# A linear-attention block gated by a squared-ReLU MLP: more matmuls on constants in the waits of the head

## The chip, the cores and the metric

The kernel runs on one core of a Trainium2 chip. The metric is device time in microseconds (us), the median of several executions; lower is better.

## The reference

One token sequence of 2048 rows and 448 columns, in bf16. It is normalised (layer norm without scale), and the result goes into two branches whose product is added to the input:

```python
xn = layernorm(x)                                   # x: 2048 x 448
q, k, v = split(xn @ wqkv)                          # 16 heads of 28
phi = lambda t: where(t > 0, t + 1, exp(t)) + 1e-6
kv  = einsum("bhsd,bhse->bhde", phi(k), v);  z = sum_s phi(k)
s   = (phi(q) @ kv) / (phi(q) @ z + 1e-6) @ wo
g   = silu(relu(xn @ w1 + b1) ** 2 @ w2 + b2)       # 448 -> 1792 -> 448
out = x + s * g
```

## The kernel before, in words

The rows are 16 tiles of 128 tokens, in four groups of four tiles. The kernel is a list of operations with the buffers that each reads and writes. A planner (`Program.schedule`) runs through them with a cost in us for each: TensorE (PE) and the DMA queue SP keep the order of the list; VectorE (DVE), ScalarE (ACT) and GpSimd (POOL) are ordered by the planner's due times, and some of their operations may go to either of two engines. The planner also gives each PSUM buffer (`Buf`) one of the eight banks, the one that is free first. Then each engine gets its instructions with the semaphore waits that the buffers ask for.

The body of the work, from about 13 us on, is a stream of PE matmuls: H (`hh`, line 786: xn times w1, per group and 128 hidden columns), K and Q (lines 729 and 739), G (lines 1092 and 1109: squared hidden times w2), and the attention's small products. The change is ahead of that, in the head, where PE waits for the first tiles:

- DMAs bring x of tile 0 (SP), tile 1 (ACT's queue), tiles 2 and 3, then w_k in four pieces, then w1 in three column ranges (0 to 511, 512 to 1279, 1280 to 1791; each as one main transfer and two for the last 64 rows), x of tiles 4 to 7 after the second, then w_q.
- Layer norm of a tile: DVE statistics (`ln_stats`, lines 483 and 484, giving `st` and `mv`), ACT Ln and Exp (`ln_rstd`, lines 491 and 495), DVE subtract and scale (`ln_norm_first` for tile 0 in two pieces, line 503; `ln_norm`, line 525), giving `xn`.
- PE transposes of xn against an identity (`pe_transpose`, line 602), in pieces of up to three blocks of 128 columns, each copied out of PSUM to `xT` by ACT (line 613) or DVE (line 612). The last 64 columns of two tiles go together (`pe_transpose_rests`, lines 627 and 637).
- K of tiles 0 and 1 in parts (`k_part`, line 801, one matmul of 128x448 for each block; `k_rests`, line 816, for the last 64 columns), and the first two hidden blocks of group 0 in parts (`head_part`, line 829; `head_rest`, line 845). `bias_cols` (line 1234) transposes b1.
- The matmuls on constants: `warm(n, after)` multiplies `dum`, a 128x128 tile of zeros, by itself n times into a PSUM bank of its own that nobody reads. With `after` the group waits for the buffers named. The planner counts 0.075 us for each.

The order of PE in the head is the order of these calls:

```python
warm(30)
warm(4, [("mv", 0)])
pe_transpose(0, ((0, 1, "act"), (1, 3, "dve")))
k_part(0, 0, 1)
k_part(0, 1, 3)
pe_transpose(1, ((0, 3, "act"),))
pe_transpose(2, ((0, 3, "dve"),))
k_part(1, 0, 3)
```

After them come the transposed rests of tiles 0 and 1, the bias, `head_part` on tiles 0 and 1, the transposes of tile 3, `k_rests`, the rests of tiles 2 and 3, `head_part` on tiles 2 and 3, `head_rest`, and then the stream of line 786.

Of the kernel before, what the change touches and what calls it, by code (L numbers as in the profile page):

```python
# [46 lines left out]
class Program:  # L47
# [6 lines left out]
    def add(self, eng, emit, reads=(), writes=(), dur=0.2, alts=(), nbytes=0, mode=None, label="", slow=1.0):  # L54
        op = Op(eng, emit, reads, writes, dur, alts, nbytes, mode, label)
        op.slow = slow
        for t in op.reads:
            op.raw.add(self.writer[t])
            self.readers.setdefault(t, []).append(op)
        for t in op.writes:  # L60
            w = self.writer.get(t)
            if w is not None and w is not op:
                op.deps.add(w)
            for r in self.readers.get(t, ()):
                if r is not op:
                    op.deps.add(r)
            self.writer[t] = op
            self.readers[t] = [r for r in self.readers.get(t, ()) if r is op]
        op.raw.discard(op)
        op.deps |= op.raw  # L70
        for d in op.deps:
            d.succ.append(op)
        self.ops.append(op)
        return op
# [231 lines left out]
def bass_recurrent_scan__linear_attn_block__dense_activation_squared_relu__prompt_kernel(  # L306
    nc, A_x, A_wqkv, A_wo, B_x, B_w1, B_b1, B_w2, B_b2, out
):
    with ExitStack() as es:
# [28 lines left out]
        mv = sb("mv", [P, NT, 2], f32)  # L338
# [255 lines left out]
        def pe_transpose(si, pieces):  # L594
            for lo, hi, eng in pieces:
                b = Buf("T")

                def f(e, _, lo=lo, hi=hi, b=b):
                    v = ps(b)[:, :].bitcast(bf)
                    last = None  # L600
                    for c in range(lo, hi):
                        last = e.transpose(v[:, (c - lo) * P : (c - lo + 1) * P], xn[:, si, c * P : (c + 1) * P], ident[:, :])
                    return last

                src = ("xf" if (si, hi) == (0, 1) else "xn", si)
                add("pe", f, [src, "ident"], [b], 0.0558 * (hi - lo), mode="128", label=f"T{si}.{lo}")

                def ev(e, eng, lo=lo, hi=hi, b=b):
                    src = ps(b)[:, 0 : 64 * (hi - lo)].bitcast(bf)
                    dst = xT[:, si, lo:hi, :].rearrange("p c k -> p (c k)")  # L610
                    if eng == "dve":
                        return e.tensor_copy(dst, src)
                    return e.activation(out=dst, in_=src, func=AF.Copy)

                n = hi - lo
                add(
                    eng, ev, [b], [("xT", si, c) for c in range(lo, hi)],
                    0.15 + 0.07 * n if eng == "dve" else 0.18 + 0.107 * n, label=f"eT{si}.{lo}",
                ).prio = -30
# [178 lines left out]
        def k_part(si, lo, hi):  # L798
            def f(e, _):
                for c in range(lo, hi):  # L800
                    last = e.matmul(  # L801
                        ps(k_head[si])[:, 0:D], xT[:, si, c, :], w_k[:, c, :], start=(c == 0), stop=False, skip_group_check=True
                    )
                return last

            add(
                "pe", f, [("wk", c) for c in range(lo, hi)] + [("xT", si, c) for c in range(lo, hi)] + ([k_head[si]] if lo else []),
                [k_head[si]], (hi - lo) * MM(D), mode="128", label=f"K{si}.{lo}",
            )
# [403 lines left out]
        def warm(n, after=()):  # L1213
            b = Buf("W")

            def f(e, _):
                last = None
                for _i in range(n):
                    last = e.matmul(ps(b)[:, 0:P], dum[:, 0:P], dum[:, 0:P], start=True, stop=True)
                return last  # L1220

            add("pe", f, ["dum", *after], [b], n * 0.075, mode="128", label="warm")
# [13 lines left out]
            )  # L1236
            add("act", lambda e, _: e.activation(out=b1f[:, :], in_=ps(bb)[:, 0 : NF // 2].bitcast(bf), func=AF.Copy), [bb], ["b1f"], 0.2, label="b1f")

        warm(30)
        warm(4, [("mv", 0)])  # L1240
        pe_transpose(0, ((0, 1, "act"), (1, 3, "dve")))
        k_part(0, 0, 1)
        k_part(0, 1, 3)
        pe_transpose(1, ((0, 3, "act"),))
        pe_transpose(2, ((0, 3, "dve"),))
        k_part(1, 0, 3)
        pe_transpose_rests(0)
# [135 lines left out]
```

## Time and profile before

| | |
|---|---|
| median of 3 runs | 147.61 us (147.25 to 147.79) |
| the profiled execution | 147.9 us, of which the span of its instructions is 146.1 |
| PE busy | 140.1 us (96%), 1177 matmuls |
| DVE, ACT, POOL busy | 102.4 (70%), 80.2 (55%), 6.3 us (4%) |
| DMA | 12.89 MB, mean 88 GB/s |
| mean granted clock of PE | 0.988 |
| chain that ended last | PE 91%, DVE 4%, DMA 2%, ACT 1% |

The span is the time from the first to the last instruction in one profiled execution. Start times below are us from its beginning. "PEclk" is the share of PE's full clock that was granted. A matmul's duration includes its way through the array, so back-to-back matmuls overlap in the records: their spacing, not their duration, is what each costs. Rows of DMAs give the time from issue to landing.

### The profile page before, as it was taken

To read this page: it belongs to the slowest core of one execution; us is meant where nothing else is said; L and a number is where in the kernel's file an instruction comes from. 1 tells how busy PE (TensorE), PEld (TensorE's weight loads), DVE (VectorE), ACT (ScalarE), POOL (GpSimd) and SP (SyncE) were. 2 spreads that over 40 slices of the span, in tenths; PEclk is the share of its full clock that TensorE was granted. 3 is DMA by queue.
4 is the path that set the end of the run, shared out by engine and by line. 5 is a ranking of instruction groups with operands and counts; after the bars stand their busy time and mean duration, and the time that the engine had idled before them with its cause. 6 is when DMAs were issued, how large, how long until landed. Compare 5 with 4: busy or idle time off the path is not lost.

```text
span 146.1 us, 3000 instructions
## 1 busy us (share of the span) xinstructions
PE 140.1 (96%) x1177; PEld 70.0 (48%) x1177; DVE 102.4 (70%) x222; ACT 80.2 (55%) x148; POOL 6.3 (4%) x40
## 2 busy tenths in 40 slices
PE   7599999999999999999999999999999999999991
PEld 7355444554444444444444444444546455555471
DVE  0943999879678899939789788963032745874874
ACT  3447997304488735597878557888417540301311
POOL 7900000000000000000000000000000000000000
PEclk9969999999999999999999999999999999999999
DMA  4899994559233100132200000000397000323032
GB/s 142 232 236 291 300 349 103 82 113 303 49 52 51 27 0 0 18 49 45 36 4 0 0 0 0 4 0 11 105 215 191 8 0 7 98 87 99 31 116 73
DMA packets 23515, 12.89 MB, mean 88 GB/s; under 512 B 14290, under 2 KB 22734, under 8 KB 23502
## 3 DMA queue, kind: packets, MB, share of 16 engines
q1 hardware_dynamic: 21842, 11.46, 30.7%
q10 hardware_dynamic: 1660, 1.25, 3.6%
q8 instruction: 9, 0.15, 0.5%
q14 instruction: 4, 0.03, 0.1%
HBM read 9.23 MB, written 1.90 MB: 76 GB/s over the span
## 4 chain that ended last, share of the span: by engine, by line
PE 91%; DVE 4%; DMA 2%; ACT 1%; issue 0%
PE pb L786 28%; PE pb L1109 19%; PE pb L1092 7%; PE pb L1184 7%; PE pb L887 6%; PE pb L729 6%; PE pb L739 6%; PE pb L1149 3%; DMA x_tok<-in_A_x_dram 2%; PE pb L829 2%; PE pb L866 1%; DVE st L483 1%; DVE gbuf L1173 1%; PE pb L893 1%; PE pb L1036 1%; PE pb L801 1%
## 5 line engine op out<-in xcount | busy, mean ns | idle before, releaser
L786 PE MATMUL pb<-xT,w 64*128 64x512 bf16 x378 | 43.6, 376 | 0.0
L764 ACT ACTIVATE r<-pb,b1f 128x512 bf16<-128x512 f32 x39 | 25.3, 685 | 15.4 <-PE pb L786 15.3
L786 PEld LDWEIGHTS pb<-xT,w 64*128 64x128 bf16 x378 | 18.0, 94 | 22.6 <-issue 1.1
L1109 PE MATMUL pb<-w,r 128*128 128x448 bf16 x140 | 27.7, 353 | 0.0
L1109 PEld LDWEIGHTS pb<-w,r 128*128 128x128 bf16 x140 | 13.2, 98 | 13.9 <-issue 1.2
L776 ACT ACTIVATE r<-r 128x1024 bf16<-128x1024 bf16 x17 | 17.8, 1062 | 0.7 <-DVE r L761 0.5
L761 DVE TENSOR_SCALAR r<-pb,b1f 128x512 bf16<-128x512 f32 x17 | 12.4, 746 | 6.0 <-PE pb L786 6.0
L1082 DVE TENSOR_TENSOR gbuf<-pb,b2b 128x448 bf16<-128x448 f32 x14 | 8.5, 618 | 5.8 <-PE pb L1109 4.3
L1204 DVE TENSOR_TENSOR gbuf<-pb,gbuf 128x448 bf16<-128x448 f32 x14 | 8.1, 618 | 6.1 <-PE pb L1184 6.1
L1092 PE MATMUL pb<-w,r 64*128 64x448 bf16 x112 | 11.7, 349 | 0.0
L729 PE MATMUL pb<-w_k,xT 64*128 64x448 bf16 x98 | 11.6, 349 | 0.0
L739 PE MATMUL pb<-xT,w_q 64*128 64x512 bf16 x84 | 11.0, 376 | 0.0
L483 DVE BATCH_NORM_STATS2 st<-x_tok 128x6 f32<-128x448 bf16 x16 | 9.1, 608 | 2.6 <-DMA x_tok<-in_A_x_dram 2.6
L1132 ACT ACTIVATE gbuf<-gbuf 128x448 bf16<-128x448 bf16 x14 | 7.0, 570 | 6.8 <-DVE gbuf L1082 5.9
L1184 PE MATMUL pb<-w_k,pqT 64*128 64x448 bf16 x96 | 10.5, 349 | 0.0
L887 PE MATMUL pb<-pk,xn 128*128 128x448 bf16 x48 | 9.6, 353 | 0.0
L1000 DVE TENSOR_TENSOR pqT<-pqT,xT 128x2048 bf16<-128x2048 bf16 x3 | 3.7, 1223 | 8.2 <-DMA xT<-scr 8.2
L719 DVE SCALAR_TENSOR_TENSOR pk<-pb,pk 128x448 bf16<-128x448 f32 x16 | 9.3, 617 | 0.1
L923 DVE TENSOR_TENSOR zacc<-zacc,pk 128x448 f32<-128x448 f32 x13 | 8.1, 620 | 0.2
L712 DVE TENSOR_SCALAR pk<-pk 128x448 bf16<-128x448 bf16 x16 | 4.1, 274 | 5.7 <-ACT pk L707 5.6
L707 ACT ACTIVATE pk<-pb 128x448 bf16<-128x448 f32 x16 | 7.8, 545 | 0.6 <-PE pb L729 0.6
L1092 PEld LDWEIGHTS pb<-w,r 64*128 64x128 bf16 x112 | 5.4, 94 | 5.3 <-issue 0.4
(99 smaller groups left out, 142.3 us busy)
## 6 DMA issues: line engine op xcount, KB each, us to landing
out_dram<-gbuf SPq DMA_DIRECT2D x15, 112.0 KB, 1.7
w<-in_B_w_dram SPq DMA_DIRECT2D x1, 1568.0 KB, 10.4
x_tok<-in_A_x_dram SPq DMA_DIRECT2D x3, 448.0 KB, 6.6
xT<-gbuf SPq DMA_DIRECT2D x32, 32.0 KB, 2.0
w<-in_B_w_dram SPq DMA_DIRECT2D x2, 384.0 KB, 5.8
xT<-scr SPq DMA_DIRECT2D x6, 112.0 KB
w<-in_B_w_dram SPq DMA_DIRECT2D x1, 576.0 KB, 6.6
xT<-scr ACTq DMA_DIRECT2D x5, 112.0 KB
```

The costliest lines, as they stand in the source:

```text
L483: add("dve", lambda e, _: e.bn_stats(st6[:, si, :], x_tok[:, si, :]), [("x", si)], [("st", si)], 0.61, label=f"bn{si}").prio = hp(si, 0)
L719: lambda e, _: e.scalar_tensor_tensor(out=slot, in0=ps(buf)[0:rows, 0:n], scalar=1.0 + 1e-6, in1=slot, op0=ALU.add, op1=ALU.max),
L729: return e.matmul(ps(b)[:, 0:D], x_tile(rows, si, c), w_k[rows, c, :], start=start, stop=stop)
L739: return e.matmul(ps(b)[:, 0:512], w_q[rows, c, m * P : (m + 1) * P], x_group(rows, g, c), start=start, stop=stop,)
L761: return e.tensor_scalar(out=slot, in0=ps(b)[:, 0:512], scalar1=b1f[:, fi : fi + 1], scalar2=0.0, op0=ALU.add, op1=ALU.max)
L764: return e.activation(out=slot, in_=ps(b)[:, 0:512], func=AF.Relu, bias=b1f[:, fi : fi + 1])
L776: return e.activation(out=both, in_=both, func=AF.Square)
L786: return e.matmul(ps(b)[:, 0:512], w_1[rows, c, fi * P : (fi + 1) * P], x_group(rows, g, c), start=start, stop=stop,)
L887: last = e.matmul(ps(b)[:, 0:D], xn_cols(si, c * P, (c + 1) * P), pk[:, si, :], start=(si == 0), stop=(si == NT - 1),)
L1092: return e.matmul(ps(b)[:, 0:D], r_cols(rows, fi, si), w_2[rows, fi, :], start=start, stop=stop)
L1109: last = e.matmul(ps(b)[:, 0:D], r_cols(slice(0, P), fi, si), w_2[:, fi, :], start=(fi == 0), stop=(fi == NF - 1),)
L1184: return e.matmul(ps(b)[:, 0:D], w, msb[rows, c, :], start=start, stop=stop)
```

## The change

Two of the groups of constant matmuls get longer, and two more groups are put into the head: 35 in place of 30 at the start, 7 in place of 4 behind the statistics of tile 0, 4 between the first and the second part of K of tile 0, and 6 between the transposes of tile 1 and those of tile 2. `warm` itself is as it was.

```diff
-        warm(30)
-        warm(4, [("mv", 0)])
+        warm(35)
+        warm(7, [("mv", 0)])
         pe_transpose(0, ((0, 1, "act"), (1, 3, "dve")))
         k_part(0, 0, 1)
+        warm(4)
         k_part(0, 1, 3)
         pe_transpose(1, ((0, 3, "act"),))
+        warm(6)
         pe_transpose(2, ((0, 3, "dve"),))
         k_part(1, 0, 3)
```

## The prediction

> **What bounds the kernel now.** I read the page first, then busy time by stretch, then the timeline of the head, then the transfers. The page's slices show TensorE (PE) full nearly everywhere and its granted clock full nearly everywhere, with one dip:
>
> ```profile
> PE   7599999999999999999999999999999999999991
> ...
> PEclk9969999999999999999999999999999999999999
> ```
>
> A slice is 3.65 us. PE is the end of the chain (91% of it), so what delays PE in the head delays the end. The 6 in the third slice is where the change works. Busy time by stretch, cut where the clock changes (quarter-microsecond stretches put the fall at 8.19 and the rise at 11.60, 3.41 us apart; I cut the other stretches to the same grid):
>
> ```profile
> core 0: us, PE busy (x) PEld busy (x) DVE busy (x) ACT busy (x) POOL busy (x), PEclk, DMA share, GB/s
> 1.36:4.78 3.42, 3.08 (x29) 2.81 (x27) 1.16 (x3) 1.28 (x1) 3.22 (x23) 1.00 0.77 211
> 4.78:8.19 3.41, 1.82 (x13) 0.88 (x13) 3.19 (x11) 2.27 (x9) 2.23 (x12) 1.00 0.88 233
> 8.19:11.60 3.41, 3.38 (x18) 2.12 (x18) 0.92 (x4) 1.05 (x5) 0.00 (x0) 0.50 0.91 256
> ...
> 141.31:144.72 3.41, 1.88 (x21) 1.59 (x19) 2.12 (x8) 1.13 (x3) 0.00 (x0) 1.00 0.36 119
> ```
>
> The clock is the number after POOL. PE is hardly idle at half clock (3.38 of 3.41 us): there it is the limit, and the stretch can cost at most half of itself, 1.71 us. The stretch before it is the loose one. The timeline of PE (start, duration, instruction, count, idle before and releaser):
>
> ```profile
> 1.06 3.38 PE L1219 MATMUL pb<-dum 128*128 128x128 bf16 x30 [1.06 <-DVE dum L368]
> 5.01 0.40 PE L1219 MATMUL pb<-dum 128*128 128x128 bf16 x4 [0.57 <-DVE mv L484]
> 5.97 0.23 PE L602 MATMUL pb<-ident,xn 128*128 128x128 bf16 x1 [0.57 <-DVE xn L503]
> ...
> 6.59 0.35 PE L801 MATMUL pb<-w_k,xT 128*128 128x448 bf16 x1
> 7.14 0.55 PE L801 MATMUL pb<-w_k,xT 128*128 128x448 bf16 x2 [0.20 <-DVE xT L612]
> 7.53 0.33 PE L602 MATMUL pb<-ident,xn 128*128 128x128 bf16 x3
> 8.22 0.50 PE L602 MATMUL pb<-ident,xn 128*128 128x128 bf16 x3 [0.36 <-DVE xn L525]
> 8.51 1.33 PE L801 MATMUL pb<-w_k,xT 128*128 128x448 bf16 x3
> ...
> 10.11 1.46 PE L829 MATMUL pb<-xT,w 128*128 128x256 bf16 x6
> 11.36 0.45 PE L602 MATMUL pb<-ident,xn 128*128 128x128 bf16 x3
> ...
> 12.40 0.83 PE L829 MATMUL pb<-xT,w 128*128 128x256 bf16 x6
> 13.16 0.39 PE L845 MATMUL pb<-xT,w 64*128 64x512 bf16 x2
> ```
>
> The same six matmuls take 1.46 us at half clock and 0.83 at full. The 30 constant matmuls stand (3.38 - 0.31) / 29 = 0.106 us apart, the four at 5.01 (0.40 - 0.22) / 3 = 0.06: so PE really ran at half until about 4.78 (the column has no record before), was granted full speed for one stretch, lost it at 8.19 and had it again at 11.60.
>
> **The change, part by part.** No instruction of DVE, ACT, POOL or a DMA is added or moved; only PE gets work, in four waits.
>
> *35 for 30.* The 35th starts at 1.06 + 34 x 0.106 = 4.66 and ends by 4.98; the next group waits for the statistics of tile 0 until 5.01. Cost 0.
>
> *7 for 4.* Three more at 0.056 end at about 5.58; the first transpose waits for DVE until 5.97. Even at half clock they end at 5.96. Cost 0.
>
> *4 inside K of tile 0.* K's first matmul at 6.59 streams for 0.19 (two take 7.53 - 7.14 = 0.39), so the four run 6.78 to 7.00; K goes on at 7.14, when DVE has copied the rest of xT. Cost 0, spare 0.14.
>
> *6 ahead of the transposes of tile 2.* The transposes of tile 1 stream from 7.53 to 7.70, the six to 8.03; tile 2's wait for DVE's normalised rows until 8.22. Cost 0, spare 0.19. If these covers are gone (half clock), see the last rival.
>
> *Banks and order.* Two more groups take a PSUM bank each for a moment. By the list, five of the eight banks have been used when the group of 4 comes and seven when the group of 6 does, so both find a fresh one; the buffers behind them then take the banks of older fillers or of copies long done. Were one behind a copy that still runs, it would cost up to 0.2 (tile 1's copy ends at 8.38, tile 2's transposes start at 8.22). The planner counts 0.075 us for each constant matmul, and could settle DVE and ACT differently later on; I bound that by 0.7 either way (one Relu of line 764, of 0.685, earlier or later) and take 0, since the waits swallow the fillers in its plan as they do here.
>
> *The clock.* Is 4.78 to 8.19 now full enough? Counted by spacing, before it holds 4 x 0.056 constants, 6 x 0.056 transposes and 3 x 0.19 of K: 1.13 us, 33%, and the clock fell after it. The other partly filled stretch, 141.31 to 144.72, holds by spacing some 1.6 us, 48% (PE is done issuing at 142.94), and the clock did not fall after it. So, if one limit governs both, it lies between 33% and 48%. The change adds 13 x 0.056 = 0.73: 1.86 us, 54%, above it. By the page's modelled busy time the bracket is 1.82 to 1.88 us and the new value about 2.5, above it too.
> The Trainium skill (TensorE: Matmul & The Clock Gate, Part 4: PE-mode transpose) says that transposes do not count as busy in the same way. By that the new fill would be 1.52 us, 45%, inside a bracket of 23% to 48%; no row here separates the two, and the sum goes by the plain count.
>
> *What full clock from 8.19 is worth.* Transposes of tile 2 at 8.22 for 0.18; K of tile 1 from 8.44 (ACT's copy ends at 8.38) for 3 x 0.19, to 9.01; transposed rests and bias to 9.3 (before: 9.63 to 10.11, 0.48 at half; I take 0.29); six of line 829 for 0.66, to 9.97 (before 10.11 to 11.36); then tile 3's transposes at 9.97 in place of 11.36. From there the chain over ACT to line 829 takes about what it takes now (11.36 to 12.40 less some 0.12 for the half-clock transposes, so 0.92): 10.89 in place of 12.40. **1.51 us earlier**; the bound was 1.71.
>
> *What is late next.* After line 845 come eight matmuls of line 786 on the first piece of w1, then those on its second piece. The issues of its three transfers, in the timeline of SP:
>
> ```profile
> 5.73 1.77 SPq L427 DMA_DIRECT2D w<-in_B_w_dram  x3
> ```
>
> and the median time from issue to landing of the last two, in the list of DMAs:
>
> ```profile
> w<-in_B_w_dram SPq DMA_DIRECT2D x2, 96.0 KB, 6.2
> ```
>
> The third is issued at about 5.73 + 2 x 0.59 = 6.9 and lands at about 13.1. Now its first use is at 13.38 + 8 x 0.108 = 14.25, with 1.15 to spare. With 1.51 taken off it would come at 12.74, so PE waits 0.36 for it. The transfers start by SP's own pace and do not come earlier. **Kept: 14.25 - 13.1 = 1.15 us.** The third piece of w1 (in the trace it lands at 16.2; first used 48 matmuls later, at about 19.4) and w2 (lands at 23.1, used at 25.45) have room; the layer-norm of tiles 4 to 7 (14.91) is fed by a DMA and may move less than PE, but is for a use at 36.
>
> Sum: the profiled execution took 147.9 us, its span 146.1 and 1.8 around it. 147.9 - 1.15 = 146.75. It lies 0.3 above the median, so the median of 147.61 becomes 146.5.
>
> **The rivals.**
> *The clock falls all the same.* Then every filler is hidden and nothing is gained: 147.6 (147.4 to 147.9). For it: the limit may not be one fill for all places, or transposes may not count. Against: the 48% stretch.
> The Trainium skill (TensorE: Matmul & The Clock Gate, Why this matters for your kernels) asks only for no idle gap over about 3 us. By that the gaps here are no cause and fillers no cure; the trace disagrees, since the longest gap in 4.78 to 8.19 is 0.57 and the clock fell.
> *The clock holds, but the gain is lost again*, in a later wait such as the PSUM banks in the stream of line 786, where ACT and DVE are 80 to 90% busy: a gain of 0.4 to 0.7, so 146.9 to 147.2.
> *The clock holds and w1 lands in time:* the whole 1.51, 146.1.
> *Slower: the fillers run at half clock.* If the stretch up to 4.78 is not enough to raise the clock, everything stays at half until 11.60. Then K's first matmul ends at 6.97, four fillers of 0.106 at 7.40 (0.26 late), K's two at 8.14, the transposes at 8.46 and six fillers at 9.10: tile 2's transposes come 0.88 late, of which half is got back once the clock rises. Plus 0.44 to 0.88: 148.0 to 148.5. It decides if the grid of stretches falls so that the constants fill only part of one. Against: 84% fill sufficed here, and the four runs lie within 0.65 us.
> The Trainium skill (same page, Part 1: The HAM clock gate) calls that grid free-running, not tied to the kernel's start; one trace cannot show it.
>
> **How the numbers follow.** 0.5% of 147.61 is 0.74 us, about what a measurement of this kernel can tell from no change. Clock holds and 1.15 is kept: 0.55. Whole 1.51: 0.08. Both are faster: 0.63. Holds but lost again: 0.09, and falls all the same: 0.17, both within 0.5%: 0.26. Slower: 0.11. The range reaches from the whole gain, 146.0, to the clock falling all the same, 147.8; it leaves out the slower case and some edges. The likeliest case by itself is 146.1 to 146.8.
>
> **What would show it.** Right: granted clock 1.00 from 8.19 on and the third slice at 9; six matmuls of line 829 at about 9.3 in 0.83; tile 3's transposes near 10.0; an idle time of PE of some 0.36 before line 786 that a DMA of w ends, near 13.1; 145 as span. Wrong: a stretch at 0.50 anywhere in the first 15 us, tile 2's transposes later than 8.25, or idle time of PE before line 786 ended by ACT or DVE.

## The result and the profile after

The changed kernel takes 146.81 us (median of 7 executions, 146.6 to 147.21) against 147.61 for the kernel before (147.25 to 148.5). The ratio is 0.9946, 95% interval 0.992 to 0.9971: 0.5% faster. The profiled execution took 147.21 us with a span of 145.0 (before: 147.9 and 146.1). All ratios here leave out executions that lie more than 1.5% above the fastest of their kernel (four of the kernel before, one of the start-only kernel); medians and counts keep them.

The page's slices, PE busy and granted clock, no longer have the dip in the third slice:

```profile
PE   7998999999999999999999999999999999999991
...
PEclk9999999999999999999999999999999999999999
```

The timeline of PE in the head:

```profile
1.05 4.66 PE L1219 MATMUL pb<-dum 128*128 128x128 bf16 x42 [1.05 <-DVE dum L368]
5.64 0.79 PE L602 MATMUL pb<-ident,xn 128*128 128x128 bf16 x3
6.29 0.36 PE L801 MATMUL pb<-w_k,xT 128*128 128x448 bf16 x1
6.49 0.39 PE L1219 MATMUL pb<-dum 128*128 128x128 bf16 x4
6.82 0.55 PE L801 MATMUL pb<-w_k,xT 128*128 128x448 bf16 x2
7.21 0.33 PE L602 MATMUL pb<-ident,xn 128*128 128x128 bf16 x3
7.37 0.50 PE L1219 MATMUL pb<-dum 128*128 128x128 bf16 x6
7.90 0.34 PE L602 MATMUL pb<-ident,xn 128*128 128x128 bf16 x3
...
9.02 0.83 PE L829 MATMUL pb<-xT,w 128*128 128x256 bf16 x6
9.68 0.33 PE L602 MATMUL pb<-ident,xn 128*128 128x128 bf16 x3
...
11.58 1.03 PE L786 MATMUL pb<-xT,w 64*128 64x512 bf16 x8
13.11 2.12 PE L786 MATMUL pb<-xT,w 64*128 64x512 bf16 x18 [0.51 <-DMA w<-in_B_w_dram]
```

All 42 constants run 0.107 apart, so at half clock; the first K at 6.29 is the first matmul at full clock (0.36 us, as in the profile before). Tile 3's transposes come at 9.68 in place of 11.36, and then the stream of line 786 stops for the second piece of w1, which lands at 13.07. That is the only wait of PE after 8 us, in the list of waits (total, times, longest):

```profile
PE pb L786 <- DMA w<-in_B_w_dram: 0.5, 1, 0.5
```

From 13.11 on PE is some 1.13 us earlier than before (where the same matmul, the ninth of line 786, ran at 14.25; the last matmul of all comes at 141.82 in place of 142.94), which is the 1.1 us of the spans. DVE, ACT and SP have the same instructions in the same order as before.

One thing differs from the picture of the prediction: here the clock rose at 6.31, not at 4.78. The edges of the stretches lie elsewhere: 6.31 is 1.54 us after 4.78, and a stretch is 3.41 long. Ten more profiles below rise at ten other places. So one profile of the kernel before shows one case of several, and the experiments had to look at many executions. In the tables below, a mean clock of 0.988 marks an execution in which the clock rose and fell again for one stretch (0.5 x 3.41 / 146 = 0.012). Half clock ahead of the first rise is not in that mean (the record begins with the rise); it shows in the spacing of matmuls and in the span.

### The profile page after: what moved, and what is told of

The parts are those of the page before. It is cut to its first block, busy times and chain, and to the rows that moved or that the text cites. A ratio compares the mean times of both kernels' runs of the same rounds, so it can differ in the third digit from the quotient of the medians.

```text
span 145.0 us, 3036 instructions
## 1 busy us (share of the span) xinstructions
PE 140.3 (97%) x1195; PEld 70.9 (49%) x1195; DVE 102.2 (70%) x222; ACT 80.2 (55%) x148; POOL 6.6 (5%) x40
## 4 chain that ended last, share of the span: by engine, by line
PE 88%; DMA 4%; SPq 4%; DVE 1%; issue 0%
PE pb L786 28%; PE pb L1109 19%; PE pb L1092 7%; PE pb L1184 7%; PE pb L887 6%; PE pb L729 6%; PE pb L739 6%; DMA w<-in_B_w_dram 4%; SPq L427 4%; PE pb L1149 3%; PE pb L866 1%; DVE gbuf L1173 1%; PE pb L893 1%; PE pb L1036 1%; PE pb L961 1%; PE pb L1062 1%
## 5 line engine op out<-in xcount | busy, mean ns | idle before, releaser
L1109 PEld LDWEIGHTS pb<-w,r 128*128 128x128 bf16 x140 | 13.1, 98 | 13.9 <-issue 1.2
L719 DVE SCALAR_TENSOR_TENSOR pqT<-pb,pqT 128x512 bf16<-128x512 f32 x12 | 7.7, 681 | 0.0
```

The source lines that it names most:

```text
L719: lambda e, _: e.scalar_tensor_tensor(out=slot, in0=ps(buf)[0:rows, 0:n], scalar=1.0 + 1e-6, in1=slot, op0=ALU.add, op1=ALU.max),
L1109: last = e.matmul(ps(b)[:, 0:D], r_cols(slice(0, P), fi, si), w_2[:, fi, :], start=(fi == 0), stop=(fi == NF - 1),)
```

## The experiments

The runs below fall into three sets, each compared with executions of the kernel before from the same set: 29, 29 and 23, together 81, median 147.63. In the column of the clock one execution of the kernel before at 0.985 is counted with those at 0.988.

| kernel | executions | mean clock 0.988 | span 146.4 or more | span 145.4 or less |
|---|---|---|---|---|
| before (30, 4) | 81 | 25 | 19 | 9 |
| changed (35, 7, 4, 6), two runs | 17 | 0 | 0 | 16 |
| start only (35, 7), two runs | 18 | 0 | 1 | 15 |
| 35 and 4 only | 12 | 5 | 1 | 5 |
| middle only (30, 4, 4, 6) | 12 | 0 | 0 | 8 |
| middle as transposes | 12 | 1 | 0 | 3 |
| no constants at all | 12 | 0 | 6 | 0 |

### The longer start alone

```diff
-        warm(30)
-        warm(4, [("mv", 0)])
+        warm(35)
+        warm(7, [("mv", 0)])
```

> 35 and 7 constant matmuls, none in the middle. Theory A (a stretch of the clock's grid falls back to half when it is filled too little, and the fillers of the middle lift it): the middle is as loose as before (with 7 for 4 the stretch 4.78 to 8.19 would be filled 39% by spacing, against 33%), so half-clock stretches stay in most executions: mean clock 0.985 to 0.995, 147.0 to 147.7 us. Rival B (what pays is the longer start, which raises the clock surely by about 4.8 or 6.3): clock 0.998 or more and the whole gain, 146.8 us.

Measured: 146.79 us, ratio 0.9934 (0.9908 to 0.9961), no execution at 0.988. The whole gain, and this was rival B's number, not mine. Six executions were few, so it ran again in the third set:

> 35 and 7 at the start and nothing in the middle, once more, for more executions. Open is whether the fillers of the middle do anything beside the longer start. With 7 the loosest stretch after a rise (4.78 to 8.19) is filled to 38% by spacing; stretches of 32 and 33% let the clock fall, 48 and 49% held it. If the limit lies under 38%: no execution at a mean clock of 0.988, 146.8 us as in the first such run, and the middle is not needed. If it lies above: some of ten executions show 0.988 and spans of 145.8, median up to 147.2 us.

Measured: 146.94 us, ratio 0.9944 (0.9918 to 0.997), again none at 0.988. One of these 12 has a span of 147.2 at a clock of 0.998, longer than the 146.7 that the latest rises below give; the kernel before has one such too, and what made them is open. The middle's fillers are not needed beside the longer start, as far as 18 executions show; a difference between the two kernels of less than about 0.2% would not show here.

### The middle alone

```diff
         k_part(0, 0, 1)
+        warm(4)
         k_part(0, 1, 3)
         pe_transpose(1, ((0, 3, "act"),))
+        warm(6)
         pe_transpose(2, ((0, 3, "dve"),))
```

> 4 and 6 constant matmuls in the middle, 30 and 4 at the start as before. Theory A: no half clock after the first rise when the grid lies as in the profile of before: clock 0.997 or more, 146.8 to 147.1 us; where the grid lies as in the profile of after (edges at 2.90 and 6.31), 30 and 4 fill 2.90 to 6.31 to only some 54% and the rise may come a stretch later. Rival B: no gain, 147.5 us.

Measured: 147.08 us, ratio 0.9962 (0.9935 to 0.9989), none at 0.988, but four of 12 spans over 145.4. Its profile caught one of those (span 145.9). The timeline of PE:

```profile
5.03 0.61 PE L1219 MATMUL pb<-dum 128*128 128x128 bf16 x4 [0.59 <-DVE mv L484]
...
7.00 0.63 PE L1219 MATMUL pb<-dum 128*128 128x128 bf16 x4
7.43 0.95 PE L801 MATMUL pb<-w_k,xT 128*128 128x448 bf16 x2
8.18 0.53 PE L602 MATMUL pb<-ident,xn 128*128 128x128 bf16 x3
8.50 0.85 PE L1219 MATMUL pb<-dum 128*128 128x128 bf16 x6
9.14 0.53 PE L602 MATMUL pb<-ident,xn 128*128 128x128 bf16 x3
...
10.60 0.83 PE L829 MATMUL pb<-xT,w 128*128 128x256 bf16 x6
```

Everything is at half clock until 9.97. This is the delay of the prediction's slower rival, tile 2's transposes at 9.14 in place of 8.22; but with 147.68 us this execution takes no longer than the kernel before does in the median. The stretch from 3.15 to 6.56 held the end of the 30, the four and two transposes, 50% by spacing, and the clock did not rise after it. So two things cost time in the kernel before: a fall after a loose stretch, and a late rise. The middle heals the fall (none at 0.988 in 12 executions, against 25 of 81); the longer start heals both.

### Which part of the start

```diff
-        warm(30)
+        warm(35)
         warm(4, [("mv", 0)])
```

> 35 in place of 30, the 4 and the middle as before. By the limits that the runs so far leave, the five more make the rise earlier in part of the executions (fewer spans of 146.6 and more), but the stretch of 4.78 to 8.19 stays at 33 to 34%, as loose as the one that let the clock fall: 0.988 in a quarter of the executions or more, median 147.3 us (147.0 to 147.6). If the three more behind the statistics do nothing: as with 35 and 7, 146.8 us.

Measured: 147.59 us, ratio 0.9982 (0.9951 to 1.0012), five of 12 at 0.988, as expected, and slower than the 147.3 that I put on it. So it is the three more constants behind the statistics of tile 0 that keep the clock: 5 of 12 with 4, none of 12 with 7 in the same set (none of 18 in both). By spacing they would lift the stretch 4.78 to 8.19 from 33% to 38%. No kept profile has a stretch as loose as that with the clock held: the two of the start-only kernel hold 52 and 66% in the first stretch after their rises, and an execution meets the loosest one only at some positions of the grid.

### No constants

Both calls of `warm` are left out.

> No constant matmuls at all. Theory A2: PE's first work comes at 5.97, so no stretch is full enough before one that begins after about 6.3, and the rise comes at 9.7 to 13.2 in every execution; spans 145.6 to 146.9, times 147.4 to 148.7, median 148.1 us, and no fall afterwards (clock 0.997 or more). Rival (the clock rises with the first real matmuls, fillers matter little): 147.5 us as before.

Measured: 148.17 us, ratio 1.0019 (0.9994 to 1.0044), spans 145.7 to 146.7. The rise at 12.33 in the profile is the latest of all profiles here. All 34 constants of the kernel before together bought some 0.5 us in the median, and by the interval of the ratio perhaps nothing; 35 and 7 buy 1.2 to 1.4 (from another set). Busy time by stretch in this kernel, at the rise and at the end:

```profile
core 0: us, PE busy (x) PEld busy (x) DVE busy (x) ACT busy (x) POOL busy (x), PEclk, DMA share, GB/s
5.50:8.92 3.42, 2.94 (x13) 1.25 (x14) 2.50 (x9) 2.01 (x8) 1.58 (x7) 1.00 0.78 225
8.92:12.33 3.41, 3.41 (x17) 1.80 (x15) 0.59 (x2) 0.84 (x4) 0.00 (x0) 1.00 1.01 313
...
142.04:145.45 3.41, 1.32 (x16) 1.09 (x14) 2.04 (x7) 0.75 (x2) 0.00 (x0) 1.00 0.33 102
```

(The 1.00 of the first two rows is the missing record.) The first stretch, 67% by spacing, did not raise the clock; the second did. The last, 34% (14 matmuls 0.0825 apart), let it fall. There are no transposes in it. From the rise at 12.33 to this fall at 145.45 are 133.12 us, 39 stretches of 3.413: the grid holds over the whole execution.

### Transposes as fillers

```diff
-        warm(4)
+        warm_t(4)
...
-        warm(6)
+        warm_t(6)
```

with 30 and 4 at the start; `warm_t` transposes the tile of zeros against the identity.

> 30 and 4 at the start, and in the middle 4 and 6 transposes of the zeros in place of 4 and 6 matmuls. If transposes count for the clock like matmuls, as in the run with the middle's fillers alone: no execution with a mean clock of 0.988, 147.1 us. If they do not count, the middle stays loose: about a quarter of the executions at 0.988, as 8 of 29 before, 147.5 us.

Measured: 147.58 us, ratio 0.9981 (0.9951 to 1.0011), one of 12 at 0.988. The median is the one that I put on transposes that do not count, one at 0.988 lies between the two cases, and the counts do not decide: the fall is rarer than before, but the late rise is more frequent than with matmuls (nine of 12 spans over 145.4, against four), and with 12 executions each that may be chance. One stretch of its profile decides:

```profile
4.95:8.36 3.41, 2.55 (x27) 1.60 (x28) 2.96 (x9) 2.45 (x10) 2.07 (x11) 1.00 0.80 211
8.36:11.78 3.42, 3.35 (x29) 2.04 (x29) 1.02 (x4) 2.27 (x8) 0.00 (x0) 1.00 0.94 273
```

Without its 19 transposes the first holds K and the last constants, some 23% by spacing; with them some 54%. The clock held. The stretch of 4.78 to 8.19 in the kernel before holds as much of K and constants, 23%, but only 6 transposes, and after it the clock fell; it fell too after 34% without any transposes. So transposes count for holding the clock, here shown by one stretch.

### The wait for w1

The second piece of w1 is loaded as two, 256 and 512 columns; x of tiles 4 to 7 stays behind both.

```diff
-        cuts = (0, 4 * P, 10 * P, F)
+        cuts = (0, 4 * P, 6 * P, 10 * P, F)
...
-            if n == 1:
+            if n == 2:
                 load_x(4, 8)
```

> The changed kernel with the second piece of w1 (columns 512 to 1279) loaded as two: 512 to 767, then 768 to 1279. Theory A says that the gain is cut off by the landing of the second piece at 13.07: the first use then needs 256 columns alone, which land near 10.5, the idle time of 0.51 before line 786 goes, and the span falls by 0.5 to 0.66 to 144.4, the time to about 146.2 us. Rival: the stream of line 786 is held by PSUM evictions or by later transfers as well, and the time stays at 146.8; three more DMA issues (1.77 us of SP's time) could even delay w_q and w2.

Measured: 147.53 us, ratio 1.0002 (0.9973 to 1.0032): the gain is gone, which is slower than either case that I gave. The wait for w1 went as expected (its 256 columns land at 10.17 and PE goes on without a stop), but the list of waits from 10 to 26 us shows what took its place:

```profile
DVE st L483 <- DMA x_tok<-in_A_x_dram: 2.0, 1, 2.0
ACT vep L491 <- DVE mv L484: 1.7, 1, 1.7
PEld pb L786 <- ACT r L764: 1.4, 2, 0.8
```

x of tiles 4 to 7 lands at 15.30 in place of 14.06. DVE waits for it, ACT waits in its queue for DVE's statistics, the Relus queued behind that Ln come late, and PE finds its PSUM banks full. From the ninth matmul of line 786 to the last matmul PE takes 129.8 us here and 128.7 in the changed kernel.

The same split in the kernel before:

> The kernel of before with that split alone. Theory A: the second piece is not late there (lands at 13.1, used at 14.25), so nothing changes: 147.5 us within 0.3. Rival: the split itself pays, 147.0 or less.

Measured: 148.1 us, ratio 1.0045 (1.002 to 1.0069). Neither case that I gave: a loss, though nothing waited for w1. Its cause is not shown. x comes late here too (15.53), but in the kept profile, which is the fastest of the 12, PE takes 128.7 us from the ninth matmul of line 786 to the last, as long as in the kernel before; and five of the 12 spans are of 146.4 and more (19 of 81 in the kernel before), so late rises may have been more frequent by chance. For the changed kernel, where the late x is what cost the gain, I moved x between the two halves of the split (first diff line above, without the second):

> The split of the second piece of w1 again, with x of tiles 4 to 7 loaded between its two halves and not behind both. Theory A2: the split took away the wait of line 786 (0.41 to 0.66), but brought x of tiles 4 to 7 at 15.30 in place of 14.06 and with it late statistics, late Relus and new waits of PE behind them; with x first, it lands near 12.6, and the gain of the split is kept: span 144.3 to 144.6, 146.2 us. The planner orders a few DVE operations differently here, which may cost some of it. Rival: DVE and ACT cannot follow a stream that starts 0.6 earlier wherever x is: 146.8 or more.

Measured: 146.72 us, ratio 0.9919 (0.989 to 0.9949), not the 146.2 that I expected. The changed kernel ran in the same set:

> The changed kernel itself, for more executions beside the other three. Theory A2 (formed after the first four runs): the grid of the clock's stretches lies anew in each execution; a stretch raises the clock when it is filled more than some 54 to 76% by spacing, and lets it fall under some 32 to 49%; 35 and 7 make the rise sure by 6.4 at the latest, the fillers of the middle keep every later stretch above the lower limit. So no execution shows a mean clock of 0.988, spans are 144.7 to 145.4, times 146.5 to 147.1 us. Rival: the change only moves the odds, and some executions lie at 145.8 to 146.7 as a good part of those before.

Measured: 146.74 us, ratio 0.9926 (0.9899 to 0.9952), none at 0.988, 9 of 10 spans at 144.8 to 145.4. In the kernel with x first, x lands at 12.27, PE waits for nothing after 8 us, and the spans are 144.5 to 144.8, some 0.25 shorter in the median. But the time outside the span is 2.0 to 2.1 us in its eight executions, against 1.7 to 1.8 in the ten of the other kernel, and the two kernels are equal. What makes those 0.25 us I don't know; no run looked into it. In the profile of the repeat PE waits for nothing either: the second piece of w1 lands at 12.73 and is first used at 12.88. So the wait of 0.51 is not in every execution.

The profile of that repeat shows the limit of the rise best, since nothing but equally spaced constants lies in the first stretch:

```profile
0.01:3.42 3.41, 2.36 (x23) 2.37 (x24) 0.11 (x1) 1.28 (x1) 2.42 (x17) 1.00 0.44 136
3.42:6.83 3.41, 3.12 (x26) 2.37 (x25) 3.08 (x8) 1.25 (x6) 3.27 (x23) 1.00 0.81 209
```

2.36 of 3.41, 69%, and the matmuls go on at 0.107; the next stretch, 74% by spacing, is followed by full clock. Weight loads (PEld) are busy for 2.37 in both, so it is not their time that decides the rise.

## Why the prediction was right, point by point

**Bound and covers.** As forecast. No filler held PE up in the profile: the transposes of tile 0 and tile 2 come at 5.64 and 7.90, both about 0.33 earlier than before, because x landed earlier in that execution (DVE's first statistics begin at 3.30 in place of 3.58).

**The clock holds.** As forecast, in 17 of 17 executions. The reason given was right in kind, not in share. If one fill is the limit for a fall, it lies between 34% and some 50% (the forecast's 48% leaves out the last matmul of its stretch). That the start alone never fell in 18 executions speaks for the lower part, but does not settle it, since its loosest stretch of 38% may not have come up. The step "the change adds 13 x 0.056" counted ten fillers that were not needed beside the other three.

**1.51 us from full clock, 0.36 of waiting, 1.15 kept.** In the span of the profiled execution it came out: 144.95 forecast, 145.0 measured, the end of the wait 13.11 against 13.1. The terms behind it hold too. Line 786 begins at 11.58 in place of 13.38, 1.80 earlier, of which 0.33 is the earlier x; in the split kernel with x first, whose x of tile 0 came as in the kernel before, it begins at 11.90, 1.48 earlier against 1.51 forecast. The ninth matmul could have come at 12.45 by spacing and came 0.67 later, where 0.36 was forecast from 12.74; the difference is the 0.3 of x again. That w1 landed at 13.07 as forecast was partly luck: it landed at 12.73 in the profile of the repeat and at 13.43 in that of the middle alone.

**From span to median.** Here the sum was off: 1.15 forecast, 0.80 measured (0.92 in the repeat). The failed step is the sentence that the profiled execution "lies 0.3 above the median, so the median of 147.61 becomes 146.5". It took the same loss off every execution. But the fall that the profile showed happens in 25 of 81 executions. The usual case of the kernel before (47 of 81, clock at 0.997 or more and a span over 145.4) is, by its spans, a late rise; the kernel without constants, which always rises late, has the same spans of 145.7 to 146.7. No execution of the kernel before with a late rise was profiled itself, but the one with the split load has the same PE list and rises at 9.77. Its loss is another than that of the fall: the ninth matmul of line 786 comes at 13.72 there, at 14.03 and 14.42 in the profiles that rise at 9.97 and 12.33, at 14.25 in the one that falls, and between 12.88 and 13.11 in the two of the changed kernel. Nine of the 81 lose next to nothing, three of these with spans of 144.5, shorter than any of the changed kernel's (144.8 at least): the change takes losses away and makes the best execution no faster.

The forecast named the free grid of stretches only as a condition of the slower rival, and held the 0.65 us between four runs against it; it is what sets the median, and the 81 executions reach from 146.28 to 148.95. The Trainium skill (TensorE: Matmul & The Clock Gate, Part 1: The HAM clock gate) calls the grid free-running. The runs agree: two executions of one kernel rise at 6.31 and 6.83 (the changed kernel), at 5.48 and 6.37 (the start alone).

**The rivals.** The clock falling all the same did not happen. The Trainium skill's rule on idle gaps (TensorE: Matmul & The Clock Gate, Why this matters for your kernels) does not describe this head: the clock fell after a stretch whose longest gap was 0.57. The Trainium skill's rule on transposes (TensorE: Matmul & The Clock Gate, Part 4: PE-mode transpose) is not what this case shows, by the 54% stretch above. The gain being lost again in later waits did not happen here, but the split showed how near it is: 1.2 us on one transfer were enough. Fillers at half clock delayed tile 2 as forecast (0.92 against 0.88), with 30 and 4 at the start, but the 148.0 to 148.5 that was put on it did not come (147.68); the five and three more are what keeps that away.

## What to carry to other kernels

The clock of PE is decided stretch by stretch, so a head full of short waits can lose it with no long gap anywhere: add up the work in the loosest 3.4 us, wherever they begin, and put fillers in until that is well above the limit, and as many ahead of the first real work as raise the clock surely. When one profile shows a loss, look at the spans and clocks of many executions before you take it off the median. And before you pull forward the transfer that PE waits for, look at what stands behind it in the queue.

## What was not expected of the hardware

Two limits, not one: by spacing, the clock rose after stretches filled 74% and more and not after 50, 67 or 69%; it fell after 33 and 34% and held after some 50% and more. So one stretch with PE two thirds full left the clock at half, and another with PE half full kept it at full.

Three more constant matmuls of 0.056 us in a wait of 0.6 us changed the share of executions that lose a stretch from 5 of 12 to none of 18.
